# When weight conversions are issued, and three smaller moves, in a fused attention, gated network and expert kernel on one core

## The chip, the cores and the metric

The kernel runs on one core of a Trainium2 chip. The core has five engines, each with its own instruction stream, that meet only through semaphores: TensorE (PE in the profile, with its weight loads as PEld), VectorE (DVE), ScalarE (ACT), GpSimd (POOL) and SyncE (SP), which here only issues transfers. The metric is the device time of one execution in microseconds; the figure for a kernel is the median of its runs.

## The reference

Three layers follow each other, all in float32 (the weights of the second are float64 on entry):

```python
scores = scale * q @ k.T                      # 2 batches, 12 heads, 448 rows, head size 64
scores = einsum('bhij,hg->bgij', scores, w_pre)
attn = softmax(scores); attn = einsum('bhij,hg->bgij', attn, w_post)
x = (attn @ v) laid out as 896 tokens x 768
xn = x / sqrt(mean(x * x) + 1e-6) * rms_g     # gated network, 768 -> 1536 -> 768
x = (silu(xn @ w_gate) * (xn @ w_val)) @ w_out
e = argmax(x @ gate)                          # 8 experts, one per token, 768 -> 1024 -> 768
out = p(e) * sigmoid(x @ output_gate)[e] * (relu(x @ w1[e]) @ w2[e])
```

## The kernel before, in words

Every large product of the second and third layer is made from three products of rounded parts (`mm3`, lines 532 to 534): each float32 operand is cast to a high part in the PE's float32r form (by ScalarE) and the rest is subtracted out as a low part (by VectorE); high times high, high times low and low times high are summed in PSUM.

*Prologue and attention.* The prologue loads q and k and turns them round by products with an identity matrix (lines 128 and 149). Ahead of these stand six products of the identity with itself that nobody reads (`self.warm(self.NW[0])`, line 1044, products at line 434). Then 90 blocks of 120 rows (10 queries by 12 heads) follow. Block m runs `pre` (head mixing, PE line 181), a row maximum (DVE, line 185), the exponential (ACT, line 191), `weigh` (DVE, lines 198 to 200, which divides the second mixing matrix by the row sums) and two blocks later `post` (PE line 211, which reads `weigh`'s tile w), a copy (ACT line 213) and the product with v (PE line 226). The order of all this is written out by hand under `manual_schedule`. Beside given blocks, the table `at(m, ...)` puts conversions of the gated network's first weights.

*Gated network.* Its 1536 columns are done in 12 chunks `fc`. A float64 weight tile becomes float32 by a transfer and four instructions: DVE 519, DVE 520, ACT 523, DVE 524 (`f64_to_f32`); ACT and DVE at line 556 split it. `whole_w(fc + 1)` does this for the gate and value tiles of the next chunk, `convert_wo(k)` for one piece of the output weights (its result goes to a tile `wor`). Both are called in the loop of line 1162, outside the hand-written stretch: there a scheduler places instructions, and it may put them as early as their tiles are free, among the attention's too. `issue_after(i)` keeps an instruction behind instruction i in its own engine's queue and does nothing more. `last["xa"]` and `last["xv"]` are the cast (ACT, line 501) and the subtraction (DVE, line 504) that split the last piece of x, the attention's normalised output.

*The seam between the two.* `tail` writes out the attention's end. Three fills (`fill[0]` to `fill[2]`, 18 products each) are products of the first half of x's rows that can run while the last piece of x is normalised. That normalisation is a chain: square (ACT 457), `total` (DVE 460), `mean` (PE 465, a sum over partitions), `power` (DVE 468, ACT 469 and 470), `newton` (DVE 473 to 476), `scale` (DVE 479), then the split at 501 and 504. After it the products of x's second half begin.

*Experts.* The 8 experts' weights come in tiles of 128x1536 (`feed`, line 960, SP's queue). `weights()` takes four tiles: ACT casts the high part wh (line 976), DVE subtracts the low part wl (line 977); `WB` names instructions behind which the n-th tile's two are kept. The low parts live in a pool "lo" (two tiles) and in four places of w0. `mm1` makes the hidden row h, `transpose_h` turns it (line 1005), `mm2` the output. The last six experts' order depends on the tokens counted: `plan_order` (lines 735 to 753) writes it to the tile `ord`, and SP reads `ord` before it issues those experts' loads (`value_load`, line 1232). The last token tile's routing (`route`, lines 663 to 727) and the first expert's x (lines 838 to 843) come just before.

Of the kernel before, what the change touches and what calls it, by code (L numbers as in the profile page):

```python
# [20 lines left out]
class Attention:  # L21
# [5 lines left out]

    SH, LP = 5, 2

    def __init__(self, tc, ctx, ps, ident, xT, nat, sp, klo, on_chunk, beside, before, tail, q, k, v, w_pre, w_post):  # L30
        self.tc, self.nc, self.ident, self.xT = tc, tc.nc, ident, xT
        self.q, self.k, self.v, self.wpp = q, k, v, (w_pre, w_post)
        self.on_chunk, self.psum, self.beside, self.before, self.tail = on_chunk, ps, beside, before, tail
        B, H, S, D = q.shape
        self.B, self.H, self.S, self.D = B, H, S, D
        self.NP = H // 2
        self.CP = 112
        self.NC = S // self.CP
        self.IB = 10
        self.QB = 120  # L40
        self.R = self.IB * H
        self.chunks = []
        for b in range(B):
            i0 = 0
            for ni in (120, 110, 110, 108):
                self.chunks.append((b, i0, ni))
                i0 += ni
            assert i0 == S
        self.blocks = []
        for n, (b, i0, ni) in enumerate(self.chunks):  # L50
            for r0 in range(0, ni, self.IB):
                self.blocks.append((n, min(r0, ni - self.IB)))
        tp = lambda name, bufs, **kw: ctx.enter_context(tc.tile_pool(name=name, bufs=bufs, **kw))
        self.nat, self.klo = nat, klo
        self.atp = tp("a_at", 2)
        self.pb = tp("a_p", 4)
        self.dp = tp("a_d", self.SH + 1)
        self.sp = sp
        self.qp = tp("a_q", 2)
        self.kp_ = tp("a_k", self.NP)  # L60
        self.sm = tp("a_sm", 4)
        self.one = tp("a_one", 1)
        self.kn, self.vn, self.kt, self.qn, self.qt = {}, {}, {}, {}, {}
        self.st, self.dt, self.pt, self.at = {}, {}, {}, {}
        self.flip = 0
        self.marks = {}
# [167 lines left out]
    def prologue(self):  # L234

        sp, pool = self.nc.sync, self.nc.gpsimd
        self.load_q(0)
        for j, f in enumerate(self.load_kv(0, "k")):
            f(pool if j % 2 else sp)
        self.load_w()  # L240
        self.load_q(1)
        self.q_part(0, 0, "av")()
        self.k_pair(0, 0, "pm")()
        for p in range(self.NP):
            if p + 1 < self.NP:
                self.k_pair(0, p + 1, ("pm", "po")[(p + 1) % 2])()
            if p == 0:
                self.q_part(0, 1, "av")()
                self.load_q(2, pool)
            for f in self.qk(0, p):  # L250
                f()
        for m in range(self.SH):
            self.shuffle(m)
        self.q_part(1, 0, "av")()
        self.q_part(1, 1, "qk")()
        for p in range(self.NP):
            for f in self.qk(1, p):
                f()
            if p == 1:
                self.build_kron()  # L260
# [74 lines left out]
class Net:  # L335
    def __init__(self, tc, ctx, args):
        self.tc, self.nc = tc, tc.nc
        (self.q, self.k, self.v, self.w_pre, self.w_post, self.wg, self.wv, self.wo, self.g,
         self.rg, self.rog, self.w1, self.w2, self.out) = args
        self.NT, self.DM = self.out.shape  # L340
        self.DF = self.wg.shape[1]
        self.E, _, self.F = self.w1.shape
        self.KD, self.KF, self.K1 = self.DM // 128, self.DF // 128, self.F // 128
        self.TT = self.NT // 128
        self.groups = ((0, 448), (448, 448))
        self.YW = self.DM + 2
        self.XT = self.TT - 1
        self.NS = 2
        self.WB = {3: ("fa", "fv"), 4: ("fa", "fv")}
        self.TK = 1  # L350
        self.NW = (6, 4, 4)
        self.PB = 6
        self.MC = 32
        self.ROOM = 14
        self.NHL = 6
        self.nstep = 0
        self.WS = 6
        self.LO = lambda nc: nc.vector
        tp = lambda name, bufs, **kw: ctx.enter_context(tc.tile_pool(name=name, bufs=bufs, **kw))
        self.cp = tp("const", 1)  # L360
        self.pq = tp("pq", 3, space=PSUM)
        self.pp = tp("pp", 2, space=PSUM)
        self.pa = tp("pa", 1, space=PSUM)
        self.dram = tp("dram", 1, space=bass.MemoryType.DRAM)
        self.ctx = ctx
        self.w0ctx = ctx
        self.last = {}
# [662 lines left out]
    def run(self):  # L1030
# [52 lines left out]
        def tail(avs, todo):  # L1083
# [6 lines left out]
            def gen():  # L1090
# [13 lines left out]
                k = [s.__name__ for s in steps].index("total") + 1  # L1104
                yield from steps[:k]
                yield cs[2][1]
                yield steps[k]
                yield steps[k + 1]
                yield fill[1]
                yield fill[2]  # L1110
                yield from steps[k + 2:]
                yield from cs[3]
            return gen()

        with ExitStack() as actx:
            a = Attention(tc, actx, self.psum, self.ident, self.xT, self.nw, sp, self.w0, self.norm, beside, before, tail,
                          self.q, self.k, self.v, self.w_pre, self.w_post)
            NB = len(a.blocks)
            self.NCH = len(a.chunks)
# [41 lines left out]
        last = KF - 3  # L1161
        for fc in range(2, KF):
            self.ffn1(fc, 0, w)
            with ExitStack() as s:
                if fc == 2:
                    for g in ("xa", "xv"):
                        s.enter_context(tc.issue_after(self.last[g]))
                w2 = self.whole_w(fc + 1) if fc + 1 < KF else None
            if fc >= last:
                for k in range(len(self.wo_s), min(WS, (fc - last + 1) * -(-WS // 3))):  # L1170
                    self.wo_s.append(self.split_wo(k, wo_raw[k]))
            while len(wo_raw) < KF * (fc - 1) // (last - 1) and fc <= last:
                wo_raw.append(self.convert_wo(len(wo_raw)))
            if fc > 3 and zeros:
                zeros.pop(0)()
            self.ffn1(fc, 1, w)
            w = w2
# [31 lines left out]
        self.raws = [[self.pool(m2, f"raw{i}", n)] * n for i, n in enumerate((1, 2, 2, 5, 2, 2))]  # L1209
        self.raws = [p for i in (3, 0, 1, 2, 4, 5) for p in self.raws[i]]  # L1210
        self.nraw = 0
        self.xp = self.pool(m2, "xp", 2)
        self.mp = self.pool(m2, "mp", 2)
        self.lo = [(self.pool(m2, "lo", 2), "wl")] * 2 + [(self.w0, t) for t in ("rawg", "rawv", "wg", "wv")]
        self.nlo = 0
        self.raw = []
        S = self.NS
# [1 line left out]
        order = list(range(S))  # L1219
        todo = [t for first, p in steps[:2 * S] for t in self.pieces(first, p)]  # L1220
        self.feed(todo, self.ROOM)
        with tc.issue_after(self.last["v"]), tc.issue_after(self.last["t"]):
            self.plan_order()
        xs.append(self.load_x(1))
        ms = [self.load_meta(p) for p in range(S)]
        hs = {}
        for n, (first, p) in enumerate(steps):
            w = self.weights()
            if first:
                x = nxt  # L1230
                if p + 2 < E:
# [73 lines left out]
```

## Time and profile before

| | |
|---|---|
| median of 3 runs | 748.62 us (747.34 to 750.33) |
| the profiled execution | 749.5 us, of which the span is 747.7 us |
| mean granted TensorE clock | 0.984 of full speed |
| attention, with the prologue | 0 to about 300 us |
| gated network, first and second product | about 300 to 460, to 568 us |
| experts | about 568 to 747 us |

Times inside the program are counted from the start of the span. The trace's rows give a start, a busy time and, in brackets, how long the engine had been idle before and what ended that idle time. A granted clock of 1.00 is 2.4 GHz and one of 0.50 is 1.2 GHz; a window's figure is the mean over it.

### The profile page before, as it was taken

Reading aid. Unit: us, or ns where it says so; the run is one execution under the profiler, and the core shown is the slowest. Engines: PE = TensorE matmul, PEld = TensorE weight load, DVE = VectorE, ACT = ScalarE, POOL = GpSimd, SP = SyncE. Lnnn points to the kernel's source line nnn. Section 1 sums busy time; section 2 is a strip of 40 time slices with the busy share of each in tenths; the row PEclk is TensorE's granted clock in tenths of the full one; section 3 lists DMA queues with packets and bytes.
Section 4 is the critical chain, followed back from the end, with each engine's and each line's share of the span. In section 5 each row is a group of like instructions: output and inputs, shape, how many; then the busy total and the mean of one; then the engine's idle time right before and its main releaser. Section 6 shows DMA issues by size and latency. Waiting matters only on the chain. (4 is left out here: it accounts for less than half of the span.)

```text
span 747.7 us, 12129 instructions
## 1 busy us (share of the span) xinstructions
PE 709.0 (95%) x4486; PEld 586.7 (78%) x4486; DVE 483.3 (65%) x1029; ACT 394.0 (53%) x692; POOL 85.3 (11%) x133
## 2 busy tenths in 40 slices
PE   8799999999996998999999999999998999999994
PEld 5466676766665777899999999999997888888774
DVE  4555668576886774889787764032214999888660
ACT  4456666566665662534343442043216888788661
POOL 4043200121000100000000000001010040100010
PEclk9999999999998999999999999999999999999998
DMA  7588746567675603877455200534237999999300
GB/s 131 105 160 166 127 79 94 101 133 144 128 159 143 155 13 127 174 249 242 137 170 169 84 1 1 211 106 148 74 135 251 335 382 382 382 377 377 116 26 19
DMA packets 83340, 121.75 MB, mean 163 GB/s; under 512 B 20867, under 2 KB 63511, under 8 KB 83279
## 3 DMA queue, kind: packets, MB, share of 16 engines
q1 hardware_dynamic: 75471, 98.05, 44.2%
q0 software_dynamic: 6656, 19.76, 12.5%
q10 hardware_dynamic: 1152, 3.15, 1.2%
q8 instruction: 37, 0.61, 0.3%
q14 instruction: 24, 0.20, 0.1%
HBM read 90.22 MB, written 11.91 MB: 137 GB/s over the span
## 5 line engine op out<-in xcount | busy, mean ns | idle before, releaser
L977 DVE TENSOR_TENSOR wl<-raw,wh 128x1536 fp32r<-128x1536 f32 x64 | 110.8, 1756 | 18.2 <-ACT wh L976 18.1
L211 PEld LDWEIGHTS ps_po<-w,p 120*112 120x112 f32 x720 | 84.5, 179 | 44.0 <-issue 30.0
L191 ACT ACTIVATE p<-ps_pm,mx 120x448 f32<-120x448 f32 x90 | 57.1, 635 | 87.9 <-DVE mx L185 48.1
L211 PE MATMUL ps_po<-w,p 120*112 120x120 f32 x720 | 94.0, 274 | 8.6 <-DVE w L200 5.6
L976 ACT CAST wh<-raw 128x1536 fp32r<-128x1536 f32 x64 | 94.2, 1479 | 11.3 <-PE ps_po L534 6.3
L185 DVE TENSOR_REDUCE mx<-ps_pm 120x1 f32<-120x448 f32 x90 | 56.1, 623 | 57.7 <-PE ps_pm L181 57.7
L181 PE MATMUL ps_pm<-d,a_kpre 120*120 120x448 f32 x180 | 86.2, 562 | 4.5 <-DMA d<-s 3.9
L523 ACT ACTIVATE raw<-raw 128x768 f32<-128x768 f32 x36 | 32.8, 920 | 72.5 <-DVE raw L520 68.2
L213 ACT COPY at<-ps_po 112x480 f32<-112x480 f32 x90 | 51.0, 567 | 2.4 <-PE ps_po L211 2.4
L175 POOL DMA_DIRECT2D d<-s x42 | 24.8, 591 | 207.6 <-PE ps_pm L181 146.7
L226 PE MATMUL ps_av<-at,v 112*64 112x110 f32 (+2 forms) x720 | 43.3, 268 | 1.2 <-ACT at L213 0.7
L533 PE MATMUL ps_po<-wl,hh 128*128 128x384 f32 x128 | 43.8, 342 | 0.0
L532 PE MATMUL ps_po<-wh,hh 128*128 128x384 f32 x128 | 43.7, 342 | 0.0
L167 PE MATMUL ps_qk<-kt,qt 64*110 64x448 f32 (+2 forms) x192 | 41.2, 410 | 2.5 <-ACT s L88 2.2
L534 PE MATMUL ps_po<-wh,hl 128*128 128x384 f32 x128 | 43.4, 340 | 0.0
L639 DVE TENSOR_TENSOR hl<-h,hh 128x1536 fp32r<-128x1536 f32 (+2 forms) x9 | 12.4, 1401 | 47.7 <-ACT hh L638 47.7
L167 PEld LDWEIGHTS ps_qk<-kt,qt 64*110 64x110 f32 (+2 forms) x192 | 18.4, 173 | 31.4 <-issue 20.1
L532 PE MATMUL ps_pm<-wh,xh 128*128 128x512 f32 x96 | 39.2, 408 | 1.5 <-ACT wh L976 1.5
L533 PE MATMUL ps_pm<-wl,xh 128*128 128x512 f32 x96 | 38.9, 406 | 1.3 <-DVE ord L753 1.3
L226 PEld LDWEIGHTS ps_av<-at,v 112*64 112x64 f32 x720 | 35.4, 138 | 5.8 <-ACT at L213 0.9
L534 PE MATMUL ps_pm<-wh,xl 128*128 128x512 f32 x96 | 38.5, 401 | 0.0
L519 DVE TENSOR_SCALAR raw<-raw 128x768 uint32<-128x768 uint32 x36 | 20.3, 569 | 24.7 <-DMA raw<-in_moe_w_gate_dram 9.2
(279 smaller groups left out, 1640.2 us busy)
## 6 DMA issues: line engine op xcount, KB each, us to landing
raw<-in_moe_w_dram SPq DMA_DIRECT2D x64, 768.0 KB
d<-s SPq DMA_DIRECT2D x48, 210.0 KB
raw<-in_moe_w_gate_dram SPq DMA_DIRECT2D x12, 768.0 KB
raw<-in_moe_w_val_dram SPq DMA_DIRECT2D x12, 768.0 KB
raw<-in_moe_w_out_dram SPq DMA_DIRECT2D x12, 768.0 KB
d<-s POOLq DMA_DIRECT2D x42, 210.0 KB, 5.7
ys<-z SPq DMA_DIRECT2D x8, 385.0 KB
v<-in_v_dram POOLq DMA_DIRECT2D x12, 224.0 KB, 6.9
```

Of the source, the lines that this page charges most:

```text
L167: nc.tensor.matmul(pss[e][:ni], lhsT=self.qt[n][sl, a, p, :ni], rhs=k[sl, :], start=(x == 0), stop=(x == 2),)
L181: self.marks[m, "p"] = nc.tensor.matmul(ps, lhsT=self.kpre.rearrange("p i g -> p (i g)"), rhs=self.dt.pop(m), start=True, stop=True).ins
L185: self.marks[m, "v"] = nc.vector.tensor_reduce(mx, ps, axis=AX.X, op=ALU.max, negate=True).ins
L191: self.nc.scalar.activation(p, ps, AF.Exp, bias=mx, scale=1.0, accum_out=sm)
L211: nc.tensor.matmul(ps[:, c], lhsT=p[:, c * CP:(c + 1) * CP], rhs=w, start=True, stop=True)
L213: self.marks[m + self.LP, "a"] = nc.scalar.copy(dst, ps.rearrange("p c h i -> p (c h) i")).ins
L226: nc.tensor.matmul(ps[e * D:(e + 1) * D, j, :ni], lhsT=vt[(g0 + e) // HH][:self.CP, (g0 + e) % HH, c, :], rhs=at[:, c, g0 + e, :ni], start ...
L532: nc.tensor.matmul(ps, lhsT=ah, rhs=bh, start=first, stop=False)
L533: nc.tensor.matmul(ps, lhsT=ah, rhs=bl, start=False, stop=False)
L534: self.last["t"] = nc.tensor.matmul(ps, lhsT=al, rhs=bh, start=False, stop=last).ins
L976: self.nc.scalar.copy(h, raw)
L977: self.last["v"] = self.nc.vector.tensor_sub(l, raw, h.bitcast(F32)).ins
```

## The change

Four things change. (1) In the gated network's loop every `whole_w` and every `convert_wo` is kept behind x's last cast on ACT and x's last subtraction on DVE; before, only the call of `fc == 2` was. (2) In `tail`, the step `mean` of the last piece of x comes ahead of `fill[1]` and `fill[2]` instead of behind them. (3) The experts' pool "lo" is allocated ahead of the pools xp and mp, so that it lies over the halves of the hidden tensor h; the second tile is kept behind the first expert's last x subtraction (`fv`), and `plan_order` is called after the first `weights()` instead of before it. (4) The unread products at the start are 8 instead of 6, and 2, 1 and 2 more (5 in all) stand between the first transposes of q and k.

```diff
@@ Attention.prologue
         self.q_part(0, 0, "av")()
+        self.warm(2)
         self.k_pair(0, 0, "pm")()
+        self.warm(1)
...
                 self.q_part(0, 1, "av")()
+                self.warm(2)
@@ Net.__init__
-        self.WB = {3: ("fa", "fv"), 4: ("fa", "fv")}
+        self.WB = {2: ("fv",), 3: ("fa", "fv"), 4: ("fa", "fv")}
-        self.NW = (6, 4, 4)
+        self.NW = (8, 4, 4)
@@ tail
-                yield steps[k]
-                yield steps[k + 1]
+                k2 = [s.__name__ for s in steps].index("mean") + 1
+                yield from steps[k:k2]
                 yield fill[1]
                 yield fill[2]
-                yield from steps[k + 2:]
+                yield from steps[k2:]
@@ loop over fc
-            with ExitStack() as s:
-                if fc == 2:
-                    for g in ("xa", "xv"):
-                        s.enter_context(tc.issue_after(self.last[g]))
+            with tc.issue_after(self.last["xa"]), tc.issue_after(self.last["xv"]):
                 w2 = self.whole_w(fc + 1) if fc + 1 < KF else None
...
-            while len(wo_raw) < KF * (fc - 1) // (last - 1) and fc <= last:
-                wo_raw.append(self.convert_wo(len(wo_raw)))
+            with tc.issue_after(self.last["xa"]), tc.issue_after(self.last["xv"]):
+                while len(wo_raw) < KF * (fc - 1) // (last - 1) and fc <= last:
+                    wo_raw.append(self.convert_wo(len(wo_raw)))
@@ experts
+        lo = self.pool(m2, "lo", 2)
         self.xp = self.pool(m2, "xp", 2)
         self.mp = self.pool(m2, "mp", 2)
-        self.lo = [(self.pool(m2, "lo", 2), "wl")] * 2 + [(self.w0, t) for t in ("rawg", "rawv", "wg", "wv")]
+        self.lo = [(lo, "wl")] * 2 + [(self.w0, t) for t in ("rawg", "rawv", "wg", "wv")]
...
-        with tc.issue_after(self.last["v"]), tc.issue_after(self.last["t"]):
-            self.plan_order()
...
             w = self.weights()
+            if n == 0:
+                with tc.issue_after(self.last["v"]), tc.issue_after(self.last["t"]):
+                    self.plan_order()
```

The line numbers of the changed kernel are higher by 3 at the places shown here. What the scheduler and the pools make of it is seen in the engines' queues. VectorE's queue, attention blocks 73 to 75 (sm and w belong to `weigh`; raw_2549 and raw_2550 are weights of chunk 1, raw_3567 is the first piece of w_out, raw_3659 the gate tile of chunk 4), before:

```order
L199 RECIPROCAL sm_2699<-sm_2699 120x1
L519 TENSOR_SCALAR raw_3567<-raw_3567 128x768
L200 TENSOR_SCALAR w_2726<-a_kpost_346,sm_2699 120x120
L520 SCALAR_TENSOR_TENSOR raw_2550<-raw_2550 128x768
L185 TENSOR_REDUCE mx_2757<-ps_pm_2755 120x1
L198 TENSOR_SCALAR sm_2722<-sm_2722 120x1
L520 SCALAR_TENSOR_TENSOR raw_3567<-raw_3567 128x768
L199 RECIPROCAL sm_2722<-sm_2722 120x1
L519 TENSOR_SCALAR raw_3659<-raw_3659 128x768
L200 TENSOR_SCALAR w_2764<-a_kpost_346,sm_2722 120x120
```

The same place after (raw_2559 and raw_2560 are chunk 1's):

```order
L199 RECIPROCAL sm_2709<-sm_2709 120x1
L200 TENSOR_SCALAR w_2736<-a_kpost_356,sm_2709 120x120
L523 SCALAR_TENSOR_TENSOR raw_2560<-raw_2560 128x768
L185 TENSOR_REDUCE mx_2767<-ps_pm_2765 120x1
L198 TENSOR_SCALAR sm_2732<-sm_2732 120x1
L199 RECIPROCAL sm_2732<-sm_2732 120x1
L200 TENSOR_SCALAR w_2774<-a_kpost_356,sm_2732 120x120
```

The rows of the two moved tiles are gone from here; with those of chunk 5's value tile that stood at the attention's end, they come after x's last subtraction now. The transfers that fill raw_3567 and raw_3659 keep their place in SP's queue; that of chunk 5's value tile is issued later. Next, TensorE's queue at the seam, before (ps_pm_3323 is `fill[2]`, x1 the second half of x):

```order
L533 MATMUL ps_pm_3323<-x0_2926,vhl_2843 128x448
L534 MATMUL ps_pm_3323<-x0_2926,vhl_2843 128x448
L465 MATMUL ps_av_3342<-ss_3277,ones_119 128x108
L532 MATMUL ps_pm_3411<-x1_3219,ghl_2450 128x448
L532 MATMUL ps_po_3430<-x1_3219,vhl_2480 128x448
```

The same product (its line is now 468) after; ps_qk_3292 is `fill[0]`, ps_qk_3316 `fill[1]`:

```order
L536 MATMUL ps_qk_3292<-x0_2936,vhl_2490 128x448
L537 MATMUL ps_qk_3292<-x0_2936,vhl_2490 128x448
L468 MATMUL ps_av_3314<-ss_3287,ones_119 128x108
L535 MATMUL ps_qk_3316<-x0_2936,ghl_2823 128x448
L536 MATMUL ps_qk_3316<-x0_2936,ghl_2823 128x448
```

It moved ahead by the 36 products of two fills. Last, VectorE's queue at the start of the experts, before (wl_5714, wl_5718, wl_5722 and wl_5726 are tiles 0 to 3 of the first expert):

```order
L843 TENSOR_TENSOR xl_5614<-ps_po_5552,xh_5613 128x384
L743 SCALAR_TENSOR_TENSOR pc_5694<-pc_5694,pm_5696,iom_80 128x6
L746 TENSOR_REDUCE pm_5696<-pc_5694 128x1
L747 TENSOR_SCALAR ohl_5695<-iom_80,pm_5696 128x6
L748 TENSOR_SCALAR pm_5696<-pm_5696 128x1
L750 SCALAR_TENSOR_TENSOR ord_5704<-ohl_5695,pm_5696,iota_86 128x8
L977 TENSOR_TENSOR wl_5722<-raw_5668,wh_5721 128x1536
L753 TENSOR_SCALAR ord_5704<-pm_5696 128x1
L977 TENSOR_TENSOR wl_5714<-raw_5664,wh_5713 128x1536
L977 TENSOR_TENSOR wl_5718<-raw_5666,wh_5717 128x1536
```

After (wl_5709, wl_5713, wl_5717 and wl_5721 are tiles 0 to 3; m_5584 is the first row of the last tile's routing; the rows between are that routing):

```order
L980 TENSOR_TENSOR wl_5709<-raw_5674,wh_5708 128x1536
L685 TENSOR_REDUCE m_5584<-ps_av_5574 128x1
...
L846 TENSOR_TENSOR xl_5624<-ps_po_5562,xh_5623 128x384
L980 TENSOR_TENSOR wl_5713<-raw_5676,wh_5712 128x1536
L980 TENSOR_TENSOR wl_5717<-raw_5678,wh_5716 128x1536
L980 TENSOR_TENSOR wl_5721<-raw_5680,wh_5720 128x1536
L743 MEMSET ohl_5727 128x8
```

Tile 0's low part is now ahead of the routing, tiles 1 to 3 follow x's subtraction directly, and the rows that write `ord` come later: the last of them stands behind wl_5826, the seventh low part.

## Rows read from the trace of the kernel before

**Rows 1.** page, busy us (share of the span) and instructions of each engine.

```profile
PE 709.0 (95%) x4486; PEld 586.7 (78%) x4486; DVE 483.3 (65%) x1029; ACT 394.0 (53%) x692; POOL 85.3 (11%) x133
```

**Rows 2.** waits of PE, 222 to 310 us: us in total, times, longest us.

```profile
PE ps_po L211 <- DVE w L200: 5.6, 2, 4.9
PE ps_pm L532 <- ACT x L501: 4.5, 1, 4.5
```

**Rows 3.** timeline, attention, 230 to 246 us: start, us, engine, line, work [idle before].

```profile
230.87 0.98 PE L211 MATMUL ps_po<-w,p 120*112 120x120 f32 x8
...
237.71 0.56 DVE L519 TENSOR_SCALAR raw<-raw 128x768 uint32<-128x768 uint32 x1 [5.00 <-DMA raw<-in_moe_w_gate_dram]
...
243.18 0.98 PE L211 MATMUL ps_po<-w,p 120*112 120x120 f32 x8
...
245.84 0.98 PE L211 MATMUL ps_po<-w,p 120*112 120x120 f32 x8
```

**Rows 4.** timeline, end of attention, 286 to 301 us.

```profile
286.69 1.38 DVE L460 TENSOR_REDUCE ss<-sq 128x108 f32<-128x648 f32 x1 [0.79 <-ACT sq L457]
...
288.53 0.37 PE L532 MATMUL ps_qk<-x,ghl 128*128 128x448 f32 x1
...
295.97 0.36 PE L465 MATMUL ps_av<-ss,ones 128*128 128x108 f32 x2
...
300.85 0.74 PE L532 MATMUL ps_pm<-x,ghl 128*128 128x448 f32 x1 [4.51 <-ACT x L501]
```

**Rows 5.** timeline, start of the experts, 568 to 596 us.

```profile
568.97 0.17 DVE L682 TENSOR_REDUCE m<-ps_av 128x1 f32<-128x8 f32 x1 [11.43 <-PE ps_av L673]
...
572.19 0.50 PE L532 MATMUL ps_pm<-wh,xh 128*128 128x512 f32 x1
...
574.23 0.49 PE L532 MATMUL ps_pm<-wh,xh 128*128 128x512 f32 x1 [1.55 <-ACT wh L976]
...
575.96 8.42 DVE L977 TENSOR_TENSOR wl<-raw,wh 128x1536 fp32r<-128x1536 f32 x5
...
576.03 0.50 PE L533 MATMUL ps_pm<-wl,xh 128*128 128x512 f32 x1 [1.30 <-DVE ord L753]
...
595.81 0.39 PE L532 MATMUL ps_pm<-wh,xh 128*128 128x512 f32 x1
```

**Rows 6.** timeline, prologue, 1 to 11 us.

```profile
1.48 2.93 PE L434 MATMUL ps_qk<-ident 128*128 128x128 f32 x12 [1.48 <-POOL ident masks.py:199]
...
6.07 0.86 PE L149 MATMUL ps_av<-ident,qn 120*128 120x120 f32 x3 [1.65 <-DMA qn<-in_q_dram]
...
7.95 1.01 PE L128 MATMUL ps_po<-ident,k 112*128 112x112 f32 x4
...
10.72 0.60 PE L128 MATMUL ps_pm<-ident,k 112*128 112x112 f32 x4
```

**Rows 7.** windows: stretch, length, busy PE PEld DVE ACT POOL, PEclk, DMA, GB/s.

```profile
230.00:246.00 16.00, 11.09 (x84) 8.17 (x83) 9.60 (x22) 8.97 (x17) 1.15 (x2) 0.79 0.46 100
285.00:305.00 20.00, 15.49 (x69) 13.76 (x70) 12.52 (x23) 7.34 (x12) 0.78 (x1) 0.91 0.36 125
300.00:460.00 160.00, 159.15 (x776) 146.67 (x777) 123.61 (x190) 65.11 (x87) 0.78 (x1) 0.99 0.47 143
326.00:341.00 15.00, 15.00 (x75) 13.79 (x74) 14.79 (x23) 6.93 (x9) 0.00 (x0) 1.00 0.78 258
568.00:586.00 18.00, 14.93 (x75) 11.90 (x74) 14.12 (x33) 12.53 (x16) 1.38 (x3) 0.91 0.76 244
596.00:656.00 60.00, 60.00 (x320) 52.53 (x319) 56.34 (x84) 48.97 (x51) 15.81 (x5) 1.00 1.06 382
```

**Rows 8.** groups of VectorE, 300 to 460 us: count | busy, mean ns | idle before.

```profile
L520 DVE SCALAR_TENSOR_TENSOR raw<-raw 128x768 uint32<-128x768 uint32 x29 | 27.6, 956 | 0.6
L524 DVE SCALAR_TENSOR_TENSOR raw<-raw 128x768 uint32<-128x768 uint32 x18 | 17.0, 955 | 3.1 <-ACT raw L523 3.1
L519 DVE TENSOR_SCALAR raw<-raw 128x768 uint32<-128x768 uint32 x29 | 16.4, 571 | 15.9 <-DMA raw<-in_moe_w_out_dram 7.0 <-DMA raw<-in_moe_w_val_dram 4.6 <-DMA raw<-in_moe_w_gate_dram 4.2
```

More of the change, by code (lines that the diff above doesn't have):

```diff
@@ L28, with __init__ @@
     SH, LP = 5, 2
-    def __init__(self, tc, ctx, ps, ident, xT, nat, sp, klo, on_chunk, beside, before, tail, q, k, v, w_pre, w_post):
+    def __init__(self, tc, ctx, ps, ident, xT, nat, sp, klo, warm, on_chunk, beside, before, tail, q, k, v, w_pre, w_post):
         self.tc, self.nc, self.ident, self.xT = tc, tc.nc, ident, xT
@@ L53, in __init__ @@
         tp = lambda name, bufs, **kw: ctx.enter_context(tc.tile_pool(name=name, bufs=bufs, **kw))
-        self.nat, self.klo = nat, klo
+        self.nat, self.klo, self.warm = nat, klo, warm
         self.atp = tp("a_at", 2)
@@ L1115, in run @@
         with ExitStack() as actx:
-            a = Attention(tc, actx, self.psum, self.ident, self.xT, self.nw, sp, self.w0, self.norm, beside, before, tail,
+            a = Attention(tc, actx, self.psum, self.ident, self.xT, self.nw, sp, self.w0, self.warm, self.norm, beside, before, tail,
                           self.q, self.k, self.v, self.w_pre, self.w_post)
```

## The prediction

> **What bounds the kernel now.** I read the busy table first: TensorE works in 95% of the span and no other engine in more than 65% [rows 1]. So time can be won in two ways only, by closing the gaps between TensorE's instructions or by giving it its full clock, and any engine that is made slower is free until TensorE waits for it. Next I read what TensorE waits for, stretch by stretch, and then the granted clock there. The windows view shows the clock below full in three places inside the program, each behind a gap: 0.79 over 16 us in late attention, 0.91 over 20 us at the seam of attention and gated network, 0.91 over 18 us at the start of the experts; in the middle of the gated network it is 0.99 and among the experts 1.00, with TensorE busy 60.00 of 60.00 us there [rows 7]. The change touches exactly these three places and the prologue, so the forecast is a sum of four terms, made against the profiled execution of 749.5 us (span 747.7); the median of the runs shown lies 0.9 below it.
>
> **Attention: conversions that leave it.** The waits view gives 5.6 us of `post` waiting for `weigh`'s tile, 4.9 of it in one wait [rows 2]. The timeline says why: VectorE's queue stood still for 5.00 us at L519, the first conversion step of a gate tile whose transfer had not landed, and L200, which makes the tile that `post` needs, stood right behind it. After that wait TensorE ran at half clock for a while. The price of the whole is read from the starts of `post`: 230.87, (one between,) 243.18 and 245.84, so three steps from 230.87 to 245.84 in 14.97 us, and an undisturbed step of 2.66 us [rows 3]. Three undisturbed steps are 7.98, so the disturbance costs 7.0 us: 4.9 of wait and 2.1 of slow clock. In the new queue L519 for that tile and for the first w_out piece are gone from these blocks, and what stays there (chunk 1's conversions) is there now as well. Nothing late is next: the following `post` comes one step later for its own inputs, whose chain kept 2.66 before and after the disturbance. Bounds: 4.9 if the clock dips anyway, 7.5 if the other 0.7 of the 5.6 goes too. I take 7.0, the reading of the rows.
>
> **Where those conversions go.** Three tiles (the first w_out piece, chunk 4's gate, chunk 5's value) move behind x's last low half, each with 0.57 + 0.96 + 0.96 us on VectorE [rows 8], so 7.4 us in all, and as many steps on ScalarE. In that stretch VectorE has 123.6 us of work in 160 [rows 7], so 131 of 160 on average, but in 326 to 341 it is busy 14.79 of 15.00 us [rows 7]: it is a queue that catches up there, and TensorE had no wait all the same. The transfers of the first two keep their place in SP's queue, hence have landed by then; the third's is issued later, but its tile is wanted a whole chunk later too. I cost the move at nothing, covered by some 29 us of VectorE's idle time; a rival below prices it if that cover is gone.
>
> **The seam.** TensorE did `fill[1]` and `fill[2]` from 288.53 to 295.97, 7.44 us, then `mean`; from there to the first product of x's second half took 300.85 − 295.97 = 4.88 us, 4.51 of it idle, put down to ACT's cast of x [rows 2, 4]. The input of `mean` was ready when the total ended at 286.69 + 1.38 = 288.07, so before `fill[1]` began. With `mean` at 288.53 the chain ends at about 293.4, while the two fills keep TensorE busy until about 296.4: the wait of 4.5 is covered with 3 us to spare. The order also takes chunk 5's value tile out of VectorE's queue between total and `power`, so nothing that waits for a transfer stands in the chain. The clock: 0.91 of 20 us is 1.8 us lost [rows 7]; I take 1.6 of it back, since the low stretch stands behind this one gap. Term 6.1, bounds 4.5 (clock dips anyway) and 6.3.
>
> **Experts.** TensorE's first products wait 1.55 us for a cast and 1.30 for VectorE [rows 5]; the second is put down to `ord`, but behind it stands tile 0's low part, queued behind the routing, `plan_order` and tile 2's low part. After the change tile 0's low part is made before the last routing, where VectorE is idle for 11.43 us [rows 5], and `mm1` can go through tile 0 in both its parts (nine products) from 572.19 while VectorE makes the low parts at 8.42 / 5 = 1.68 us each [rows 5]. Tile 1's comes at about 575.1 and is needed near 574.5, so a gap of some 0.3 to 0.6 remains. Waits 2.85 − 0.5 = 2.4; the slow clock behind the two gaps is 0.09 × 18 = 1.6 [rows 7]. Term 4.0; bounds 1.3 (one wait goes, the clock stays) and 4.5. The cost on the other side: `ord` is finished after the seventh low part, some 10 us later, and SP, which reads it before it issues the third expert's loads, stands that long. Two more tiles are issued ahead of that read than before, and TensorE showed no idle time in 596 to 656 although the transfers ran at 382 GB/s [rows 7]; I take 0, with the price in a rival.
>
> The Trainium skill's page "TensorE: Matmul & The Clock Gate", section "HAM oscillation — how this bites in real kernels", speaks against the clock part of this term: it holds that the gate falls behind one long idle gap, and two gaps of 1.55 and 1.30 us, with work between them, are short ones. By that rule the fall would not hang on these gaps, and the term would be 2.4 instead of 4.0, the sum 734.4. The trace has the clock down right behind the two gaps all the same, so I keep 4.0 and the smaller figure lies within the range.
>
> **Prologue.** Twelve instructions of six unread products took 2.93 us, 0.49 each product [rows 6]. The two added at the start end near 5.4, before q lands: TensorE idles 1.65 us ahead of 6.07 [rows 6], so they are free. Five more stand between the transposes: 2.4 us at that rate if nothing covers them, and TensorE waits little there. On the other side, the same four-fold transposes take 1.01 at 7.95 and 0.60 at 10.72 [rows 6], so the engine is slow until about 10.5, and denser work may bring the full rate sooner; two us sooner give back about 1. Bounds −0.5 and +2.0 (part of the five falls into waits for k). I take +0.4, nearer to the lower end, since the first products of q and k also wait for transfers.
>
> **The sum.** 7.0 + 6.1 + 4.0 − 0.4 = 16.7; 749.5 − 16.7 = 732.8. The median stood 0.9 lower than the profiled run, so I say 732.5. The best ends give 7.5 + 6.3 + 4.5 + 0.5 = 18.8, so 730.7 (729.8 as a median); the worst 4.9 + 4.5 + 1.3 − 2.0 = 8.7, so 740.8.
>
> **Rivals.**
> (a) The experts win nothing: a stall won at their start is given back, because transfers set the end of that stage, and `ord`'s delay pushes them back. For it: the transfer engines are the fullest there, share 1.06 at 382 GB/s, and VectorE has 56.34 of 60 us [rows 7]. Against it: TensorE was the one without a gap. Time 749.5 − 12.7 = 736.8.
> (b) The attention's stall turns into another: VectorE freed of L519 runs into the next thing that is late, a shuffled tile d or another weight tile. For it: the gap was long enough to let every transfer catch up unseen. Against it: undisturbed steps of 2.66 right behind it [rows 3]. With half of the term gone, 736.3.
> (c) The slower side: the gated network's first part becomes VectorE's. At each moved tile the queue stops until a transfer lands, as it did for 5.00 us in attention [rows 3], and TensorE waits for chunk 4's weights and all that queues behind: three times (5.0 + 2.5) = 22.5 us, so 749.5 − 16.7 + 22.5 = 755.3. It decides once VectorE has no idle time left between 300 us and chunk 4's first product; for it speaks 14.79 of 15.00 busy [rows 7]; against it the 29 us of idle time in the whole stretch and two of three transfers that keep their place in the queue. To end slower than before, it must eat more than 16.7.
> (d) The change does not do what it says: the scheduler puts the conversions early all the same. The queue as shown excludes that; no chance of its own.
>
> **How the numbers follow.** The forecast with its own terms inside their bounds gets 0.78, (a) 0.08, (b) 0.06, (c) 0.04, and 0.04 is left for mishaps that take over 12 us and leave the time about unchanged. The forecast's range is 729 to 740, and (a) and (b) fall inside; what is left out is (c), the mishaps and a little beyond the bounds. A measurement of this kernel can tell about 0.5%, 3.7 us, from no change. Faster by more: 0.78 + 0.08 + 0.06 less a little for coincidence of the worst ends, 0.90; within 0.5%: 0.06; slower: 0.04.
>
> **What would show it.** Right: no wait of `post` for `weigh` above 1 us around 235 us and full clock there; no gap between `fill[2]` and the second half's products; the second expert's first product about 19.6 us behind the first expert's instead of 595.81 − 572.19 = 23.6 [rows 5]; the gated network's first part still without a wait of TensorE for VectorE; the clock up no later than 10.5 us. Wrong: a wait of TensorE for the split weights of chunks 3 or 4 (rival c), TensorE waiting for casts among the experts and their stage ending as late as before (rival a), steps of attention above 2.7 us in blocks that were smooth (rival b), or a prologue longer by over 2 us.

## The result and the profile after

| | before | after |
|---|---|---|
| median | 749.48 us of 4 runs (747.34 to 750.73) | 730.78 us of 4 runs (729.94 to 732.87) |
| ratio | | 0.9758, 95% interval 0.9724 to 0.9791 |
| profiled execution | 749.5 us | 729.94 us |
| span, mean granted clock | 747.7 us, 0.984 | 728.2 us, 0.996 |

The change made the kernel 18.7 us faster by the medians (the kernel before with one run more than was shown above); 16.7 us had been forecast. The two profiled executions differ by 19.6 us, and where that came from is read by taking the same instruction in both traces and the difference of its starts:

| instruction | before | after | ahead by | won since the row above |
|---|---|---|---|---|
| block 0's exponential | 28.15 | 27.56 | 0.59 | 0.6 (prologue) |
| block 10's exponential | 50.71 | 47.77 | 2.94 | 2.4 (first blocks) |
| block 74's exponential | 229.15 | 226.17 | 2.98 | 0.0 |
| block 78's exponential | 246.82 | 236.81 | 10.01 | 7.0 (the stall of `post`) |
| the 289th product of x with the gate and value weights | 346.26 | 330.03 | 16.23 | 6.2 (seam) |
| first product of the experts | 572.19 | 556.13 | 16.06 | −0.2 |
| last output copy | 737.66 | 718.02 | 19.64 | 3.6 (experts) |

The page's busy table after, which answers to [rows 1]: TensorE's share rose by one point, while VectorE's work stayed what it was, since nothing was taken away from it.

```profile
PE 702.1 (96%) x4500; PEld 582.5 (80%) x4500; DVE 482.0 (66%) x1029; ACT 392.9 (54%) x692; POOL 77.7 (11%) x133
```

TensorE's waits after, 206 to 294 us, which answer to [rows 2]: 4.9 and 4.5 us are gone, and nothing above 1.0 us took their place.

```profile
PE ps_po L211 <- ACT s L88: 1.0, 1, 1.0
PE ps_po L211 <- DVE w L200: 0.7, 1, 0.7
PE ps_av L226 <- ACT at L213: 0.7, 1, 0.7
```

The timeline of the same blocks after, for [rows 3]. The four starts of `post` are 2.67, 2.66 and 2.67 us apart, and an L200 has ended 1.27 us ahead of each:

```profile
230.56 0.98 PE L211 MATMUL ps_po<-w,p 120*112 120x120 f32 x8
...
231.68 0.28 DVE L200 TENSOR_SCALAR w<-a_kpost,sm 120x120 f32<-120x120 f32 x1
...
233.23 0.98 PE L211 MATMUL ps_po<-w,p 120*112 120x120 f32 x8
...
235.89 0.98 PE L211 MATMUL ps_po<-w,p 120*112 120x120 f32 x8
...
238.56 0.98 PE L211 MATMUL ps_po<-w,p 120*112 120x120 f32 x8
```

The seam after, for [rows 4]: `mean` at 278.58, x's cast at 282.68, when `fill[2]` had just begun, and its low half done at 283.44 + 0.83 = 284.27. TensorE was still in `fill[2]` then and waited for none of it.

```profile
278.58 0.36 PE L468 MATMUL ps_av<-ss,ones 128*128 128x108 f32 x2
...
282.68 0.73 ACT L504 CAST x<-xT 128x648 fp32r<-128x648 f32 x1 [2.77 <-DVE xT L482]
...
283.44 0.83 DVE L507 TENSOR_TENSOR x<-xT,x 128x648 fp32r<-128x648 f32 x1 [0.80 <-ACT x L504]
```

The start of the experts after, for [rows 5]. Tile 0's low part (the first row) is made at 550.19, ahead of the routing; `mm1` runs from 556.13 without a gap; what is new are two waits for h's halves, 0.22 us at the first four of h's transposes and 0.49 at the last four.

```profile
550.19 1.76 DVE L980 TENSOR_TENSOR wl<-raw,wh 128x1536 fp32r<-128x1536 f32 x1 [8.96 <-PE ps_po L537]
...
556.13 0.50 PE L535 MATMUL ps_pm<-wh,xh 128*128 128x512 f32 x1
...
563.51 0.66 PE L1008 MATMUL ps_qk<-ident,h 128*128 128x128 f32 x4 [0.22 <-ACT h L996]
...
567.23 0.66 PE L1008 MATMUL ps_qk<-ident,h 128*128 128x128 f32 x4 [0.49 <-ACT h L996]
...
569.68 0.14 DVE L756 TENSOR_SCALAR ord<-pm 128x1 int32<-128x1 f32 x1
...
576.12 0.39 PE L535 MATMUL ps_pm<-wh,xh 128*128 128x512 f32 x1
```

The second expert's first product is the last row, 19.99 us behind the first's; it was 23.62. `ord` is finished at 569.8, 13.7 us behind the first product.

The prologue after, for [rows 6]. The three-fold product at 5.57 takes 0.53 (0.86 before), the four-fold one at 7.20 takes 0.60 (1.01 before): TensorE has its full rate by 5.6 us, where it had it after 10 us. The row at 5.93 is the first two of the five added products.

```profile
1.49 3.70 PE L437 MATMUL ps_qk<-ident 128*128 128x128 f32 x16 [1.49 <-POOL ident masks.py:199]
...
5.57 0.53 PE L149 MATMUL ps_av<-ident,qn 120*128 120x120 f32 x3 [0.38 <-DMA qn<-in_q_dram]
...
5.93 0.62 PE L437 MATMUL ps_qk<-ident 128*128 128x128 f32 x4
...
7.20 0.60 PE L128 MATMUL ps_pm<-ident,k 112*128 112x112 f32 x4 [0.65 <-DMA k<-in_k_dram]
```

The windows after, for [rows 7], moved with the work; columns as there. The clock (the third figure from the right, ahead of the transfers' share) is full in each, VectorE's work in the gated network rose from 123.61 to 129.28 us with TensorE busy all 160.00, and the experts go on at 383 GB/s without a gap.

```profile
227.00:243.00 16.00, 15.87 (x137) 11.47 (x134) 12.47 (x31) 12.06 (x26) 1.91 (x4) 1.00 0.80 168
271.00:291.00 20.00, 20.00 (x167) 18.80 (x164) 14.13 (x28) 9.16 (x15) 0.77 (x1) 1.00 0.48 145
283.80:443.80 160.00, 160.00 (x789) 147.69 (x788) 129.28 (x198) 67.62 (x89) 0.77 (x1) 1.00 0.48 148
309.80:324.80 15.00, 15.00 (x75) 13.79 (x74) 14.85 (x23) 7.28 (x9) 0.00 (x0) 1.00 0.73 246
552.00:570.00 18.00, 17.02 (x97) 13.76 (x97) 15.35 (x36) 14.37 (x20) 1.37 (x3) 1.00 0.70 237
580.00:640.00 60.00, 60.00 (x322) 52.66 (x322) 53.86 (x84) 47.00 (x50) 7.21 (x4) 1.00 1.06 383
```

### The profile page after: what moved, and what is told of

Read it like the earlier page. It is cut to its first block, busy times and chain, and to the rows that moved or that the text cites. A ratio compares the mean times of both kernels' runs of the same rounds, so it can differ in the third digit from the quotient of the medians.

```text
span 728.2 us, 12156 instructions
## 1 busy us (share of the span) xinstructions
PE 702.1 (96%) x4500; PEld 582.5 (80%) x4500; DVE 482.0 (66%) x1029; ACT 392.9 (54%) x692; POOL 77.7 (11%) x133
## 4 chain that ended last, share of the span: by engine, by line
PE 75%; issue 9%; DMA 7%; DVE 5%; ACT 2%; SPq 1%; POOL 0%; POOLq 0%; ACTq 0%; DVEq 0%
PE ps_po L211 9%; PE ps_pm L181 8%; PE ps_po L537 5%; PE ps_pm L537 5%; PE ps_po L536 5%; PE ps_po L535 5%; PE ps_av L226 5%; PE ps_pm L536 5%; PE ps_pm L535 5%; PE ps_qk L535 4%; PE ps_qk L537 4%; PE ps_qk L536 4%; PE ps_qk L167 4%; DMA out_dram<-o,ids 4%; DMA d<-s 2%
## 5 line engine op out<-in xcount | busy, mean ns | idle before, releaser
L211 PE MATMUL ps_po<-w,p 120*112 120x120 f32 x720 | 92.4, 272 | 3.6 <-ACT s L88 2.9
L88 DVE COPY s<-ps_qk 110x448 f32<-110x448 f32 (+2 forms) x48 | 29.8, 620 | 7.7 <-PE ps_qk L167 7.3
```

The costliest lines, as they stand in the source:

```text
L211: nc.tensor.matmul(ps[:, c], lhsT=p[:, c * CP:(c + 1) * CP], rhs=w, start=True, stop=True)
```

## The experiments

All are edits of the changed kernel; ratios are to the kernel before, run on the same chip.

| kernel | median us | ratio, 95% interval |
|---|---|---|
| changed kernel | 730.78 | 0.9758 (0.9724 to 0.9791) |
| u1_conv: conversions free again | 738.17 | 0.9830 (0.9795 to 0.9865) |
| u1_gate: gate and value tiles only | 737.82 | 0.9831 (0.9795 to 0.9868) |
| u1_wo: w_out pieces only | 730.35 | 0.9724 (0.9688 to 0.9761) |
| u2_mean: mean behind both fills | 738.66 | 0.9848 (0.9812 to 0.9884) |
| m_mid: mean between the fills | 733.11 | 0.9790 (0.9761 to 0.9819) |
| u3_exp: experts' part undone | 736.47 | 0.9810 (0.9772 to 0.9848) |
| u3_plan: planning ahead again | 730.54 | 0.9752 (0.9720 to 0.9784) |
| u3_lo: old pool for low parts | 736.90 | 0.9845 (0.9818 to 0.9871) |
| u4_warm: no added products | 733.39 | 0.9786 (0.9763 to 0.9810) |
| w_front: only the two at the start | 731.73 | 0.9772 (0.9742 to 0.9803) |
| w_inner: only the five between | 731.70 | 0.9764 (0.9736 to 0.9792) |
| again: the changed kernel | 731.67 | 0.9773 (0.9746 to 0.9800) |

The medians come from four jobs on different chips, and the interval of each ratio reaches some 2 to 2.6 us to either side, so a cost that is told by medians alone is rough. Where in the program the time goes is read from the traces, as in the table of the result: the same stretch in the experiment's trace and in the changed kernel's, one execution each.

| stretch | kernel | longer than in the changed kernel's trace, us |
|---|---|---|
| block 74's to block 78's exponential | u1_conv, u1_gate, u1_wo | 7.4, 7.3, 0.7 |
| block 78's exponential to the 289th product | u2_mean, m_mid | 7.0, 1.5 |
| first expert's first product to the second's | u3_exp, u3_lo, u3_plan | 4.9, 3.6, −1.0 |

**The conversions.** The three kernels take `issue_after` from both calls, from `whole_w` alone (u1_gate) or from `convert_wo` alone (u1_wo):

```diff
-            with tc.issue_after(self.last["xa"]), tc.issue_after(self.last["xv"]):
+            with ExitStack() as s:
+                if fc == 2:
+                    for g in ("xa", "xv"):
+                        s.enter_context(tc.issue_after(self.last[g]))
                 w2 = self.whole_w(fc + 1) if fc + 1 < KF else None
...
-            with tc.issue_after(self.last["xa"]), tc.issue_after(self.last["xv"]):
-                while len(wo_raw) < KF * (fc - 1) // (last - 1) and fc <= last:
-                    wo_raw.append(self.convert_wo(len(wo_raw)))
+            while len(wo_raw) < KF * (fc - 1) // (last - 1) and fc <= last:
+                wo_raw.append(self.convert_wo(len(wo_raw)))
```

> The changed kernel, with the conversions of chunk 4's gate tile, chunk 5's value tile and the first w_out piece let back among the attention's instructions. Theory A (TensorE's gap is one wait of VectorE for a gate tile that has not landed, and the slow clock behind it): post waits some 5 us for weigh near 232 us, the clock is low behind it, and the time is 730.8 + 7.0 = 737.8. Rival B (with the rest of the change in place the attention runs earlier and the tile has landed by then, or another wait hid behind this one): less than 3.5 us come back, under 734.3.

> The changed kernel with only the gate and value tiles' conversions let back; the w_out piece stays behind x. Theory A: the wait belongs to the gate tile's transfer, so all of it comes back, 737.8, with a stop of VectorE of 5 us at that tile's first step. Rival C (what costs is the work that conversions put between weigh's steps, whichever tile they are of): the gate tile is half of it, 734.3, and no long stop for a transfer.

> The changed kernel with only the w_out piece's conversion let back into attention. Theory A: its tile has landed when VectorE comes to it (0.18 us of idle time before), so next to nothing comes back, 730.8 to 731.3. Rival C: half of it, 734.3.

u1_conv cost 7.4 us and u1_gate 7.0 by the medians, u1_wo nothing (730.35); the traces say 7.4, 7.3 and 0.7 for the blocks in question. The timeline of u1_gate has the old stall, from the gate tile alone:

```profile
231.28 0.98 PE L211 MATMUL ps_po<-w,p 120*112 120x120 f32 x8
...
236.22 0.56 DVE L522 TENSOR_SCALAR raw<-raw 128x768 uint32<-128x768 uint32 x1 [5.33 <-DMA raw<-in_moe_w_gate_dram]
...
238.69 1.94 PE L211 MATMUL ps_po<-w,p 120*112 120x120 f32 x8 [4.58 <-DVE w L200]
```

and its window there has the clock at 0.79 again, as before the change [rows 7]:

```profile
230.00:246.00 16.00, 11.43 (x91) 8.30 (x88) 8.72 (x20) 7.72 (x18) 0.57 (x1) 0.79 0.41 94
```

In u1_wo VectorE stopped at the w_out piece for 1.21 us, and `post` waited 0.44 for it:

```profile
230.32 0.56 DVE L522 TENSOR_SCALAR raw<-raw 128x768 uint32<-128x768 uint32 x1 [1.21 <-DMA raw<-in_moe_w_out_dram]
...
231.22 1.05 PE L211 MATMUL ps_po<-w,p 120*112 120x120 f32 x8 [0.44 <-DVE w L200]
```

So theory A holds: what cost was one instruction that waited for a transfer at the head of VectorE's queue, and not the conversions' work, of which u1_wo puts one tile of three back for 0.7 us instead of the 3.5 of rival C. Its tile had not quite landed there, against what the expectation took from the trace before. Rivals B and C fall.

**The seam.** u2_mean restores the order in which both fills come ahead of `mean`; m_mid puts it between them:

```diff
                 k2 = [s.__name__ for s in steps].index("mean") + 1
-                yield from steps[k:k2]
                 yield fill[1]
+                yield from steps[k:k2]
                 yield fill[2]
                 yield from steps[k2:]
```

> The changed kernel with mean's product again behind fills 1 and 2. Theory A (the chain of 4.9 us from mean to x's split is uncovered there, and the clock falls behind that gap): a wait of 4.5 us for the cast of x, a low clock behind it, 730.8 + 6.1 to 6.4 = 736.9 to 737.2. Rival D (the chain was long because a conversion stood in VectorE's queue ahead of it, which is gone now): a wait under 3 us and no low clock, under 734.

> The changed kernel with mean between fills 1 and 2, so that one fill of 3.7 us covers a chain of 4.9 us. Theory A: TensorE waits 1.2 us for the cast of x, 732.0; if one gap of that size is enough to lower the clock, 1.6 to 2.9 more, 733.6 to 734.9. Rival D (the chain is shorter now): no wait, 730.8.

u2_mean has the wait of 4.5 us back, with the chain as long as ever: from `mean` at 287.60 to the product at 292.48 are 4.88 us, as in [rows 4], and a clock of 0.76 in the window around it. It cost 7.9 us by the medians, more than the 6.1 to 6.4 expected; in the trace the seam is 7.0 us longer. The clock is part of the difference: of the 3.4 us that 0.24 of 14 us comes to, 1.3 fall into the wait, when TensorE has nothing to do, and 2.1 behind it, where the clock is 0.72 from 292.48 to 300 us; in the trace before the change 1.6 fall behind the wait (0.62 from 300.85 to 305). What is left of the 7.9 lies outside the seam or within the noise.

```profile
287.60 0.36 PE L468 MATMUL ps_av<-ss,ones 128*128 128x108 f32 x2
...
292.48 0.74 PE L535 MATMUL ps_pm<-x,ghl 128*128 128x448 f32 x1 [4.51 <-ACT x L504]
```

```profile
286.00:300.00 14.00, 9.49 (x38) 8.27 (x37) 10.38 (x24) 6.50 (x10) 0.77 (x1) 0.76 0.34 100
```

m_mid has the same chain (280.55 to 285.43, 4.88 us) under one fill, a wait of 0.79 us, and a clock that stays up:

```profile
280.55 0.36 PE L468 MATMUL ps_av<-ss,ones 128*128 128x108 f32 x2
...
285.43 0.48 PE L535 MATMUL ps_pm<-x,ghl 128*128 128x448 f32 x1 [0.79 <-ACT x L504]
```

```profile
277.00:293.00 16.00, 15.21 (x74) 13.41 (x74) 10.55 (x25) 6.52 (x10) 0.77 (x1) 1.00 0.31 90
```

Its median lies 1.4 above the changed kernel's of the same job, which is within the intervals; the seam in its trace is 1.5 us longer. Both agree with theory A's 1.2. Rival D falls: the chain is not shorter without the conversion.

**The experts.** u3_exp undoes the whole part, u3_plan only the place of `plan_order`, u3_lo only the pool (and the kept-back second tile):

```diff
# u3_plan
+        with tc.issue_after(self.last["v"]), tc.issue_after(self.last["t"]):
+            self.plan_order()
         xs.append(self.load_x(1))
...
-            if n == 0:
-                with tc.issue_after(self.last["v"]), tc.issue_after(self.last["t"]):
-                    self.plan_order()
# u3_lo
-        self.WB = {2: ("fv",), 3: ("fa", "fv"), 4: ("fa", "fv")}
+        self.WB = {3: ("fa", "fv"), 4: ("fa", "fv")}
-        lo = self.pool(m2, "lo", 2)
...
-        self.lo = [(lo, "wl")] * 2 + [(self.w0, t) for t in ("rawg", "rawv", "wg", "wv")]
+        self.lo = [(self.pool(m2, "lo", 2), "wl")] * 2 + [(self.w0, t) for t in ("rawg", "rawv", "wg", "wv")]
```

> The changed kernel with the experts' part undone: the low parts' pool at its old place and the order's planning ahead of the first weights. Theory A (two gaps of 1.55 and 1.30 us at the first expert's start, and the slow clock behind them): both gaps back, clock low behind them, 730.8 + 3.6 to 4.0 = 734.4 to 734.8. Rival E (the gaps are made up for further on, because transfers set the pace of the experts): back within 1 us, 731.8 at most.

> Pool at its new place, planning ahead of the first weights again. Theory A: tile 0's low part is still made before the routing, so the gap ahead of the first low product stays closed; the next low part comes behind the planning's first rows, some 1 us later, and one gap of about 1 us opens: 731.5 to 732, and a single short gap leaves the clock up. Rival F (the planning's rows are what holds the queue): the whole 3.6 us come back, 734.4.

> Planning at its new place behind the first weights, pool at its old place (and the second tile not kept behind x's subtraction). Theory A: the low parts of tiles 2 and 0 then follow x's subtraction, tile 0's ends some 3.4 us behind it instead of before the routing, so TensorE has gaps of about 2.5 us in sum, and the clock falls: 730.8 + 3 to 4 = 734 to 735. Rival F: the planning was the cost and it is out of the way, 731 to 732.

u3_lo, with the planning out of the way, has both gaps in full and the clock down behind them:

```profile
561.01 0.49 PE L535 MATMUL ps_pm<-wh,xh 128*128 128x512 f32 x1 [1.54 <-ACT wh L979]
...
562.80 0.50 PE L536 MATMUL ps_pm<-wl,xh 128*128 128x512 f32 x1 [1.30 <-DVE wl L980]
```

```profile
557.00:575.00 18.00, 15.14 (x73) 11.87 (x72) 14.51 (x26) 13.91 (x14) 1.18 (x2) 0.91 0.62 209
```

Its first expert takes 23.61 us from first product to first product (558.97 to 582.58), the 23.62 of before. u3_plan has one gap of 0.29 us and stands at the changed kernel's time. So the gain comes with the pool, which lets tile 0's low part be made ahead of the routing; the second tile that is kept back goes with it in u3_lo, and no run takes the two apart. Rival F falls. Moving the planning won nothing and may cost a little: with it ahead again the first expert takes 18.98 us in u3_plan's trace, against 19.99 in the changed kernel's and 19.3 to 20.2 in the other traces with pool and planning as changed, and the two waits for h's halves are gone; the medians do not show it. u3_exp has both gaps (1.59 and 1.29 us), so rival E falls too; it cost 5.7 us instead of 3.6 to 4.0, with one of its four runs at 731.48. Its trace has the clock at 0.72 over 18 us: a low stretch of 6.8 us begins in the second gap, where the trace before has one of 3.4, and another one of 3.4 us stands ahead of the first product. u3_plan and u1_conv have such a stretch ahead of the first product as well, with no gap of TensorE above 0.3 us in the ten us before it; the changed kernel's two traces don't, and the runs do not tell why.

**The unread products.** u4_warm takes out all seven, w_front the five, w_inner the two; `again` is the changed kernel itself:

```diff
# w_inner and u4_warm
-        self.NW = (8, 4, 4)
+        self.NW = (6, 4, 4)
# w_front and u4_warm
-        self.warm(2)
...
-        self.warm(1)
...
-                self.warm(2)
```

> The changed kernel without the seven unread products that were added. The trace of the changed kernel shows the full clock from 4.98 us (before: 10.48), the prologue 0.6 us shorter, and no low stretch at 41 to 44.6 us, which the kernel before had. Theory G: both belong to the added products, 730.8 + 0.6 + 2.4 = 733.8, full clock from about 10.5 us and a low stretch near 41 us. Rival H: only the 0.6 belongs to them, the low stretch near 41 us comes and goes from one execution to the next: 731.4. Rival I (the forecast): the products cost, 730.4.

> Eight unread products at the very start, none between the transposes. If the two at the start bring the rise (they end near 5.4 us instead of 4.4), the rise is near 5 to 6 us, and without the five the prologue is 0 to 1 us shorter than the changed kernel's: 730 to 731. If the five carry it, the clock rises at 10 us or later and the time is that of the kernel without all seven, 733.4.

> Six unread products at the start as before the change, and the five between the transposes. If the two at the start bring the rise: about 10 us, with five products more on the path, 733 to 734. If the five carry it: rise by 8 us, 731.

> The changed kernel once more, unaltered, with a trace of another execution. Its first trace had the full clock from 4.98 us and no low stretch before 700 us. Theory H (moment of the rise and low stretches in the first 45 us differ from one execution to the next): the rise is late, up to 10 us, or there is a low stretch between 20 and 45 us, about evenly likely; the same median within 1.5 us. Theory G (the added products settle both): rise before 6 us and no low stretch again.

The first four-fold transpose of k tells TensorE's rate near 7 us. In w_inner, w_front and u4_warm, in this order, it is slow:

```profile
7.28 0.95 PE L128 MATMUL ps_pm<-ident,k 112*128 112x112 f32 x4
```

```profile
7.08 1.01 PE L128 MATMUL ps_pm<-ident,k 112*128 112x112 f32 x4 [0.45 <-DMA k<-in_k_dram]
```

```profile
7.17 1.01 PE L128 MATMUL ps_pm<-ident,k 112*128 112x112 f32 x4 [0.52 <-DMA k<-in_k_dram]
```

and in `again` it is fast:

```profile
6.83 0.61 PE L128 MATMUL ps_pm<-ident,k 112*128 112x112 f32 x4
```

Of ten traces of kernels with all seven products nine have 0.60 or 0.61 there and one has 0.95 (u2_mean); the four traces without, or with a part of them (the kernel before among them), have 0.95 to 1.01. But this does not show that it takes both halves. In six of the ten traces the rate is up before any of the five has run: the three-fold product of q takes 0.53 us, as in the changed kernel's first trace at 5.57, and the first of the five starts behind it. Up to there these kernels have the same products as w_front, whose one trace has the three-fold product slow:

```profile
5.77 0.86 PE L149 MATMUL ps_av<-ident,qn 120*128 120x120 f32 x3 [0.50 <-DMA qn<-in_q_dram]
```

So eight products at the start can bring the rise alone and do so in some executions; in three more of the ten (`again` among them) it comes while the five run, at 6.2 to 6.8 us, and whether the five bring it there is not shown. With six at the start none of three traces has it before 10 us (10.48, u4_warm 13.98, w_inner 10.24). The low stretch near 41 us is another thing. The changed kernel had none in its first trace, 30 to 45 us, and one in `again` (the rows in this order):

```profile
30.00:45.00 15.00, 11.78 (x71) 8.30 (x70) 7.95 (x30) 8.47 (x23) 4.61 (x7) 1.00 0.79 157
```

```profile
30.00:45.00 15.00, 11.50 (x61) 8.27 (x60) 6.53 (x24) 7.43 (x20) 4.27 (x7) 0.89 0.76 146
```

Five of the ten traces with all seven have a low stretch between 20 and 45 us. Theory H holds for it; the early rise goes with the added products, as theory G has it, but not in every execution. In time, u4_warm lies 1.7 to 2.6 us above the changed kernel's two medians, with overlapping intervals: the gain of this part is seen in the traces (block 0's exponential comes 2.1 us later in u4_warm than in the changed kernel) and not settled by the medians. The difference between either half and all seven is not measurable.

## Why the prediction was right, step by step

*Attention, 7.0 us.* Measured 7.0 between blocks 74 and 78, and 7.3 to 7.4 there when the conversions are let back. Reading the price off the steps of `post`, slow clock included, was what made it exact; the waits view alone would have said 4.9.

*The moved conversions, nothing.* VectorE has 32 first steps of conversions in that stretch, where it had 29, and in its fullest part is busy 14.85 of 15.00 us; TensorE ran 160.00 of 160.00 us. Idle time ahead of the first step of a conversion fell from 15.9 us [rows 8] to 11.0, so the work went into time that had been spent waiting:

```profile
L522 DVE TENSOR_SCALAR raw<-raw 128x768 uint32<-128x768 uint32 x32 | 17.7, 567 | 11.0 <-DMA raw<-in_moe_w_out_dram 4.2 <-DMA raw<-in_moe_w_gate_dram 4.1 <-DMA raw<-in_moe_w_val_dram 2.7
```

Rival (c) is refuted, and (b) by the waits table: no other wait moved in.

*Seam, 6.1.* Measured 6.2. The chain kept its length, 5.6 us from `mean` to the end of x's low half, in every trace but that of u1_conv (6.2, with a step of a conversion in it), so the argument by cover was right, and m_mid shows where it stops.

*Experts, 4.0.* Measured 3.6 in the traces. Of the 2.85 us of gaps, 2.1 are won; the 0.5 that I kept for a gap at tile 1 turned up as 0.22 + 0.49 at h's halves. The clock part, 1.6, came as the rows had it: wherever the two gaps stood (before, u3_lo, u3_exp) the clock was low behind them, and with gaps of 0.22 and 0.49 it stayed up. By the Trainium skill's "TensorE: Matmul & The Clock Gate", section "HAM oscillation — how this bites in real kernels", two short gaps would have left the clock alone; these traces do not bear that out here. That the gaps are what made it fall is likely and not shown, since in three traces it also fell just ahead of the first product without them. One reading was off: the second gap was not a wait for tile 0's low part, which runs from 575.96 to 577.71, while the product starts at 576.03. What had just ended is tile 2's:

```profile
574.22 1.75 DVE L977 TENSOR_TENSOR wl<-raw,wh 128x1536 fp32r<-128x1536 f32 x1
```

TensorE had gone on to tile 2 while tile 0's low part was missing, and u3_lo shows the same wait put down to a low part, with no `ord` in the way. The remedy was right all the same: with tile 0's low part made early, the nine products of tile 0 come first, 556.13 to 558.46, and by then the next tile is ready. What I had not seen is which part does it: the delayed `ord` was no gain, and SP's queue, 10 us later, was hidden. Rival (a) is refuted.

*Prologue, −0.4.* This is the step that failed, in sign: "nearer to the lower end" should have been the lower end itself, −0.5. It was −0.6 in the trace. The five products do stand on TensorE's path, but the rate came back some 5 us sooner, and the products themselves ran at the full rate (0.62 us for four instructions, where 0.98 was reckoned). I had bounded that gain by a rise two us sooner.

*What was not in the sum.* 2.4 us in blocks 2 to 10. About 0.7 is waiting there (for the shuffled tiles d 3.9 us in the trace before and 2.1 after, less a new wait of 1.1 for the copy of at), and 1.7 the low stretch at 41 us that the profiled execution before had and the one after had not. The prediction counted three places with a low clock and missed this fourth one (0.83 from 36 to 46 us in the trace before). As `again` shows, the 1.7 belong to the execution. The 0.7 may too: from block 0's exponential to block 10's the changed kernel's first trace takes 20.2 us, and five traces of experiments without a low stretch there take 20.6 to 21.0.

So the mechanisms held and the sum came close, with some luck in the total: the four terms measured 7.0, 6.2, 3.6 and 0.6, 17.4 in sum against 16.7, because the errors of the last two have opposite signs. The rest of the 19.6 between the profiled executions may be a matter of which executions were profiled; the medians differ by 18.7.

## What to carry to other kernels

A conversion that a scheduler has hoisted costs what stands behind it in its engine's queue: look for the instruction that waits for a transfer right ahead of the one the busy engine needs, and price it by the pace of that engine's steps, so that the slow clock behind the gap is counted too. A chain off the main engine costs nothing if the filler put behind its start is longer than it; here 7.4 us of products cover 4.9 us, and half of them leave 0.8. Where tiles are laid over memory can decide when they are written: here moving one pool, with one tile kept back, won what re-ordering the planning did not.

## What the runs showed of the hardware that was not expected

TensorE's early rise of the clock is not the same from one execution to the next: of eleven traces with eight unread products at the start six had the full rate before 5.7 us, ahead of any of the five added ones, three rose at 6.2 to 6.8, and two at 10 or later, w_front and u2_mean; with six at the start all three rose after 10 us. A slow stretch among the first blocks can be paid back: m_mid's clock was 0.69 from 20 to 30 us, and its block 0 started 1.7 us behind the changed kernel's, yet its block 6 started 1.8 us ahead, since the waits that the changed kernel has there (3.9 us in three kinds, 2.1 of them for the shuffled tiles) were gone. A low stretch at 37 to 45 us was not paid back by block 10: those blocks took 22.1 us in `again` and 23.2 in u3_lo, against 20.2 in the changed kernel's first trace.
